# Chunked attention with a gated MLP on one core: other planned times for the w_in transfers, and a pacing limit that changes 1.5 MB later

## The chip, the cores and the metric

The kernel runs on one core of one Trainium2 chip. That core has five instruction streams that run side by side: TensorE (PE, matrix products), VectorE (DVE), ScalarE (ACT), GpSimd (POOL) and SyncE (SP, which here only issues transfers). Transfers between the chip's memory (HBM) and the on-chip buffers run on 16 DMA engines. The metric is the device time of one execution, in microseconds (us); lower is better.

## The reference

Two stages are computed, all in float32. First a chunked attention: batch 4, 8 heads, 768 positions, 64 numbers a head. Every chunk of 32 queries looks at its own 32 keys, 16 before, 8 behind, and 8 memory keys that belong to the head:

```python
scores = scale * np.matmul(q_c, k_full.transpose(0, 1, 3, 2))
scores = scores - np.max(scores, axis=-1, keepdims=True)
a = np.exp(scores)
a = a / (np.sum(a, axis=-1, keepdims=True) + 1e-09)
out[:, :, c_start:c_end] = np.matmul(a, v_full)
```

Then a gated MLP over the result x (4 x 768 x 512):

```python
h = np.maximum(x @ w_in, 0.0)                # w_in: 512 x 1024
u, v = (h[..., :d_ff // 2], h[..., d_ff // 2:])
v_n = (v - mu) / np.sqrt(var + 1e-06)        # mean and variance over v's last axis
v_s = np.einsum('ts,bsd->btd', w_spatial, v_n) + b_spatial[None, :, None]
gated = u * v_s
return (gated @ w_out).astype(np.float32)
```

The weights w_in and w_out arrive as 64-bit floats and are turned into 32-bit ones on the chip.

## The kernel before, in words

**Tiling.** The attention is cut into 24 units of 128 positions (four chunks each), all heads of a batch at once; six units make a batch. For unit i, PE forms the scores from q and a padded copy of k (`sx<-kmain,q`, L419), DVE takes the maximum and subtracts it (L476, L480), ACT takes the exponential (L485), DVE sums and inverts (L490 to L493), PE transposes the result (`pt`, L507), ACT copies it (L510), PE multiplies it by v (`sx<-vmain,pT`, L419), DVE scales (`xs`, L459), PE transposes again (`xt`, L523), and the result x is kept as a rounded high part (ACT, L528) and the rest, its low part (DVE, L532). Products of the MLP are three matmuls each, high by high, low by high and high by low (L561 to L563). Below, s2 is the score product of unit 2, mx2, p2, den2 and xs2 its steps on DVE, x2 the low part of its result, and v2 the MLP group of 12 matmuls that makes unit 2's 128 rows of v (`f<-win_h,x`); the groups that make u (`f<-x,win_h`) take three units at once.

**The weights.** w_in comes in eight pieces of 512 KB: four row blocks times two column halves (the half for v first). Each piece lands in one of four `big` buffers. Here w0 to w3 are the pieces of v's half and w4 to w7 those of u's half. A piece is converted by ACT (L864, L869), DVE (L873, L874) and POOL (L879), then split into a high part by ACT (`win_h`, L893) and a low part (`win_l`, L897) by DVE for w0 to w3 and by POOL for w4 to w7. The function `from_f64` does the conversion; it serves w_out too, whose four pieces come late in the program.

**The second half.** The normalised v and the relu of u go to HBM (`vn_far`, `u_far`) and come back for the product with w_spatial and then with w_out; both products use a scheme with seven products in place of eight (L710).

**What sets the order.** Every step is registered with the class `Plan`: its engine, an assumed duration, what it reads and writes, a rank. `Plan.order` (L76) lays all steps out in time with these assumed numbers, and the order of starts is the order of the instructions on every engine. For a transfer of mb megabytes it assumes that the one pipe for all transfers is taken for mb times drag over 0.30 us. Where PE would stand idle between 9 and 36 us of the plan, it fills the gap with matmuls on a constant (`idle<-ident`, L252), one for each 0.45 us.

**Pacing.** `held_by` (L140) says for which earlier transfer a new one waits, so that the megabytes under way stay below a limit. The same function is used for the plan and for the waits that are written into the program. Its limit is 2.0 MB until 9.0 MB have been issued, then `MIDDLE`'s 1.2 MB until 38 MB, then 1.75 MB; beyond 9.0 MB no more than eight transfers are under way either. All loads, and the stores of v and u, go through SP's one queue in program order, so a waiting transfer holds up those behind it. The third pair of q and k (for units 4 and 5) is four pieces of each.

Of the kernel before, what the change touches and what calls it, by code (L numbers as in the profile page):

```python
# [10 lines left out]
U32 = mybir.dt.uint32  # L11
# [8 lines left out]
SLOT = 40  # L20
LEFT = 16
WIN = 64
MIDDLE = (38.0, 1.2)
PIECES = 4
NEG = -1.0e30

# [1 line left out]
class Plan:  # L28
# [111 lines left out]
    def held_by(self, flight, mb, none):  # L140

        moved = sum(size for _, size in flight)
        window = self.early[1] if moved <= self.early[0] else MIDDLE[1] if moved < MIDDLE[0] else self.window
        for back, (name, size) in enumerate(reversed(flight), 1):
            mb += size
            if back == 8 and moved > self.early[0] or mb > window:
                return name
        return none
# [10 lines left out]
def tile_chunked_attention_gmlp(  # L159
# [120 lines left out]
    def transfer(e, out_, in_, mb, of=None):  # L280
        ins = e.dma_start(out=out_, in_=in_)
        made.setdefault(of, []).append(ins.ins.name)
        wait = plan.held_by(flight, mb, None)
        if wait:
            wait_for(ins, [wait], "pace")
        flight.append((ins.ins.name, mb))

    def load(dst, src_, w, rank, r=(), eng="SP", slow=1.0, us=0.45, seq=False, drag=1.0, of=None):
        e = {"SP": nc.sync, "ACT": nc.scalar, "POOL": nc.gpsimd}[eng]
        n = 4  # L290
        for s in src_.shape:
            n *= s
        mb = n / 1e6 * slow
        n = op(eng, us, lambda: transfer(e, dst() if callable(dst) else dst, src_, mb, of), r=r, w=w, rank=rank, mb=mb,
               after=line.get(eng) if seq else None, drag=drag)
        if seq:
            line[eng] = n
# [249 lines left out]
    seq = [0]  # L547
# [305 lines left out]
    def from_f64(name, src_, rank, load_rank, home, after=()):  # L853
        big = ("big", *name)
        zk = ("st", ("z", name))

        def get():
            a = alloc("big", big, [P, 2 * DH], U32).rearrange("p (c w) -> p c w", w=2)
            t_[big] = a
            return a  # L860
        load(get, src_.bitcast(U32).rearrange("p (c w) -> p c w", w=2), w=[("big", big)], r=after, rank=load_rank, seq=True)

        def scale_():
            nc.scalar.activation(alloc("st", ("z", name), [P, DH], F32), t_[big][:, :, 1].bitcast(F32), AF.Copy,  # L864
# [12 lines left out]
        def add():  # L877
# [6 lines left out]
           w=[("big", big)] if home else [zk], rank=rank)  # L884
# [17 lines left out]
    def w_in_part(c, part, rank, load_rank, sub_eng):  # L902
        cols = slice(part * DH, (part + 1) * DH)
        z, zk = from_f64(("win", c, part), w_in[c * P:(c + 1) * P, cols], rank, load_rank, False)
        split(sub_eng, DH, lambda x: (win_l if x else win_h)[:, c, cols], z, [zk], [("win", c, part)], rank)
# [31 lines left out]
    def w_out_pair(c, rank, load_rank):  # L937
        def halves(z):
            return lambda: z().rearrange("p (h n) -> p h n", h=2)

        def dst(i, x):
            third_part()
            return t_["wout"][:, i, x, c]
        (zu, ku), (zd, kd) = [from_f64(("wout", d), w_out[d * P:(d + 1) * P], 260.0, load_rank, True) for d in (c + 2, c)]
        end = [("fin", n) for n in range(count[0])]
        right_hand("wout", c, HN, halves(zu), halves(zd), [ku, *end], [kd, *end], dst, rank, "POOL", "DVE")
# [65 lines left out]
    for b in range(B + 1):  # L1012
        if b < B:
            rank = 300.0 + 10 * b
# [67 lines left out]
```

## Time and profile before

| | us |
|---|---|
| three runs | 379.18, 381.41, 376.54 |
| median | 379.18 |
| the profiled execution | 375.05 |
| its span, first to last instruction | 373.3 |
| PE busy | 355.9 (95%) |
| DVE busy | 285.0 (76%) |
| ACT busy | 187.1 (50%) |
| POOL busy | 160.5 (43%) |

The profiled execution is 4.1 us below the median of the three runs and 1.5 us below their lowest; 1.75 us of it lie outside the span. Busy times are unions over the span. The filler matmuls count as PE's busy time like any other. The granted PE clock reads full throughout. HBM moved 173 GB/s over the span.

### The profile page before, as it was taken

What the parts mean: (1) busy time and instruction counts of PE and PEld (TensorE: products, weight loads), DVE (VectorE), ACT (ScalarE), POOL (GpSimd) and SP (SyncE); (2) the same over time, 40 slices, a digit from 0 to 9 for tenths busy, and PEclk for the clock granted to TensorE, in tenths of its full rate; (3) what the DMA queues carried; (4) which work ended last, traced back from release to release, by engine and by line L of the source; (5) the groups of instructions that cost most, each with busy time, mean ns of one, the idle gap of its engine ahead of it and who ended that gap; (6) DMA issues with size and microseconds to landing.
All of it is one profiled execution on the core that took longest, in us unless ns stands there. A gap on an engine that the chain in (4) does not pass through costs nothing.

```text
span 373.3 us, 11922 instructions
## 1 busy us (share of the span) xinstructions
PE 355.9 (95%) x4988; PEld 326.7 (88%) x4988; DVE 285.0 (76%) x479; ACT 187.1 (50%) x334; POOL 160.5 (43%) x155
## 2 busy tenths in 40 slices
PE   2987989999999999999999999999999999999995
PEld 2865877998988978979889898999999999999995
DVE  3888856748758568566598589999969896898893
ACT  3768435454555454554473355346434743744371
POOL 6446642374386077520042194961256025106500
PEclk9999999999999999999999999999999999999999
DMA  8995888778787765886742648205720662230014
GB/s 230 316 260 140 232 257 210 235 217 220 228 251 214 249 212 147 274 232 194 216 163 93 246 137 311 88 2 173 246 90 3 207 217 84 84 130 2 0 54 159
DMA packets 48517, 65.52 MB, mean 176 GB/s; under 512 B 5456, under 2 KB 39888, under 8 KB 48464
## 3 DMA queue, kind: packets, MB, share of 16 engines
q1 hardware_dynamic: 47808, 64.44, 56.5%
q8 instruction: 39, 0.64, 0.8%
q10 hardware_dynamic: 656, 0.33, 0.3%
q14 instruction: 14, 0.11, 0.1%
HBM read 45.88 MB, written 18.87 MB: 173 GB/s over the span
## 4 chain that ended last, share of the span: by engine, by line
PE 83%; DVE 11%; ACT 2%; issue 2%; DMA 1%; SPq 0%; ACTq 0%; DVEq 0%
PE y L710 21%; PE f L710 15%; PE f L561 12%; PE f L562 11%; PE f L563 11%; PE sx L419 9%; PE xt L523 3%; PE pt L507 3%; DVE op L690 2%; DVE sm L673 2%; DMA k<-in_k_dram 1%; DVE st L874 1%; DVE st L873 1%; DVE wout L897 1%; DVE p L480 1%
## 5 line engine op out<-in xcount | busy, mean ns | idle before, releaser
L710 PE MATMUL y<-wsp,op 128*128 128x384 f32 x288 | 52.0, 336 | 0.9 <-ACT st L750 0.9
L764 POOL TENSOR_TENSOR ug<-st,ug 128x384 f32<-128x384 f32 x24 | 36.0, 1513 | 38.4 <-DVE st L756 34.4
L710 PEld LDWEIGHTS y<-wsp,op 128*128 128x128 f32 x288 | 49.9, 188 | 1.2 <-ACT st L750 1.2
L561 PE MATMUL f<-x,win_h 128*128 128x384 f32 x128 | 46.1, 360 | 0.0
L563 PE MATMUL f<-x,win_h 128*128 128x384 f32 x128 | 43.2, 337 | 0.0
L562 PE MATMUL f<-x,win_l 128*128 128x384 f32 x128 | 43.1, 337 | 0.0
L561 PE MATMUL f<-win_h,x 128*128 128x512 f32 x96 | 40.8, 425 | 0.0
L710 PE MATMUL f<-wsp,op 128*128 128x384 f32 x216 | 39.4, 336 | 0.0
L562 PE MATMUL f<-win_h,x 128*128 128x512 f32 x96 | 37.9, 394 | 1.0 <-DVE x L532 1.0
L563 PE MATMUL f<-win_l,x 128*128 128x512 f32 x96 | 37.7, 392 | 0.0
L710 PEld LDWEIGHTS f<-wsp,op 128*128 128x128 f32 x216 | 37.6, 188 | 0.0
L690 DVE TENSOR_TENSOR op<-sm,op 128x768 fp32r<-128x768 f32 x32 | 34.7, 1093 | 3.1 <-ACT op L687 2.6
L710 PE MATMUL y<-wout,op 128*128 128x256 f32 x288 | 35.9, 281 | 0.5 <-DVE op L690 0.5
L459 DVE TENSOR_TENSOR xs<-sx,rec 128x512 f32<-128x512 f32 x24 | 16.5, 687 | 25.1 <-PE sx L419 25.0
L710 PEld LDWEIGHTS y<-wout,op 128*128 128x128 f32 x288 | 34.7, 188 | 1.0 <-DVE op L690 0.8
L770 POOL TENSOR_TENSOR st<-st,bias 128x384 f32<-128x384 f32 x14 | 18.6, 1337 | 37.2 <-ACT st L750 28.4
L597 POOL TENSOR_TENSOR rstd<-ve,mhalf 128x1 f32<-128x1 f32 x24 | 14.7, 611 | 44.7 <-DVE ve L593 43.6
L687 ACT CAST op<-sm 128x768 fp32r<-128x768 f32 x32 | 26.2, 837 | 11.6 <-DVE sm L673 10.2
L419 PEld LDWEIGHTS sx<-kmain,q 64*32 64x32 f32 x1536 | 17.0, 107 | 14.8 <-issue 11.7
L622 ACT ACTIVATE uo<-f 128x384 f32<-128x384 f32 x32 | 15.6, 492 | 25.2 <-PE f L563 21.9
L398 POOL COPY vmain<-memv 8x1024 f32<-8x1024 f32 x22 | 23.9, 1090 | 10.0 <-PE sx L419 7.8
L419 PE MATMUL sx<-kmain,q 64*32 64x64 f32 x1536 | 20.9, 228 | 7.3 <-ACT kmain L404 7.0
(86 smaller groups left out, 770.6 us busy)
## 6 DMA issues: line engine op xcount, KB each, us to landing
vmain<-in_v_dram SPq DMA_DIRECT2D x48, 128.0 KB
vn_far<-st SPq DMA_DIRECT2D x24, 256.0 KB
u_far<-uo SPq DMA_DIRECT2D x32, 192.0 KB
vr<-vn_far SPq DMA_DIRECT2D x8, 768.0 KB
ug<-u_far SPq DMA_DIRECT2D x16, 384.0 KB
q<-in_q_dram SPq DMA_DIRECT2D x40, 128.0 KB
vmain<-in_v_dram SPq DMA_DIRECT2D x47, 96.0 KB
out_dram<-ot SPq DMA_DIRECT2D x33, 128.0 KB
```

Source lines behind the costliest of these rows:

```text
L398: ins = {"DVE": nc.vector, "POOL": nc.gpsimd}[eng].tensor_copy(to, of)
L419: ins = nc.tensor.matmul(o, w_, m, start=True, stop=True, skip_group_check=True)
L459: nc.vector.tensor_tensor(xs.rearrange("p t r d -> p r t d"), t_["sx", i][:, :, 1], rec.rearrange("p t r -> p r t").unsqueeze(3).broadcast ...
L561: nc.tensor.matmul(o, lh, rh, start=(j == 0), stop=False)
L562: nc.tensor.matmul(o, ll, rh, start=False, stop=False)
L563: nc.tensor.matmul(o, lh, rl, start=False, stop=(j == len(pairs) - 1))
L622: op("ACT", act(HT), lambda: nc.scalar.activation(alloc("uo", i, [P, HT], F32), t_["f", n], AF.Relu), r=[("f", n)], w=[("uo", i)], rank=rank)
L687: nc.scalar.copy(half(0), of())
L690: nc.vector.tensor_tensor(half(1), of(), half(0).bitcast(F32), op=ALU.subtract)
L710: nc.tensor.matmul(o, x, y, start=first and m == 1, stop=m == 3 * chunks, skip_group_check=True)
L764: nc.gpsimd.tensor_tensor(g, t_[st(x)], g, op=ALU.mult)
L770: {"DVE": nc.vector, "POOL": nc.gpsimd}[eng].tensor_tensor(a, a, bias[:, 1], op=ALU.add)
```

## The change

Two things are edited. The load of `from_f64` gets drag 0.75: the plan takes 0.524 MB x 0.75 / 0.30 = 1.31 us of the pipe for a piece of w_in or w_out, where it took 1.75. And the limit of 1.2 MB holds from 10.5 MB instead of from 9.0; between the two it is 1.75 MB. By the sizes that the plan counts, 9.05 MB have been issued when the last v of unit 3 is under way, and 10.56 MB behind the third pair of q and k and the first store of v.

```diff
-MIDDLE = (38.0, 1.2)
+MIDDLE = (10.5, 38.0, 1.2)
...
-        window = self.early[1] if moved <= self.early[0] else MIDDLE[1] if moved < MIDDLE[0] else self.window
+        window = self.early[1] if moved <= self.early[0] else MIDDLE[2] if MIDDLE[0] < moved < MIDDLE[1] else self.window
...
-        load(get, src_.bitcast(U32).rearrange("p (c w) -> p c w", w=2), w=[("big", big)], r=after, rank=load_rank, seq=True)
+        load(get, src_.bitcast(U32).rearrange("p (c w) -> p c w", w=2), w=[("big", big)], r=after, rank=load_rank, seq=True, drag=0.75)
```

No instruction of the computation is added or taken away. The order changes on every engine from the first microseconds until the last unit of attention; from the first product of the second half on, DVE's order is the same again. The first 26 transfers of SP's queue, down to the v of unit 3, stand as before; behind them the four pieces of q of the third pair now come ahead of the first store of v, which was ahead of them, and k's four pieces follow that store as they did.

On PE, at its first filler matmuls, up to the first MLP group (`idle` is the filler, `pt`, `xt` and `sx` as named above):

```order
 L419 MATMUL sx<-kmain_148,q 32x64 x32
 L507 MATMUL pt<-ident,p 128x128 x4
-L252 MATMUL idle<-ident 128x256 x13
-L507 MATMUL pt<-ident,p 128x128 x4
-L419 MATMUL sx<-vmain,pT 32x64 x32
-L252 MATMUL idle<-ident 128x256 x2
-L523 MATMUL xt<-ident,xs 128x128 x4
-L252 MATMUL idle<-ident 128x256 x3
-L419 MATMUL sx<-kmain_147,q 32x64 x32
```

In the changed program ten fillers stand at the place of the thirteen, four at the places of the two and the three, and none at the place of a single one further on: 17 in all (with three ahead of this place, the same in both) in place of 22. The first attention product now stands ahead of unit 1's transpose.

On DVE, from unit 0's x on, before (`win_l` from st_316 is w3's low part; st_442 with big_322 is w4):

```order
L532 TENSOR_TENSOR x_391<-xt_380,x_391 128x4x128
L897 TENSOR_TENSOR win_l_109<-st_316,win_h_108 128x512
L476 TENSOR_REDUCE mx_444<-sx_401 128x8
L873 TENSOR_SCALAR st_442<-st_442 128x512
L874 SCALAR_TENSOR_TENSOR st_442<-big_322,st_442 128x512
L480 TENSOR_TENSOR p_460<-sx_401,mx_444 128x2x4x64
L490 TENSOR_REDUCE den_498<-p_460 128x8
```

and in the changed program (w3 is st_313, w4 is st_431 with big_315):

```order
L532 TENSOR_TENSOR x_382<-xt_369,x_382 128x4x128
L476 TENSOR_REDUCE mx_438<-sx_397 128x8
L873 TENSOR_SCALAR st_431<-st_431 128x512
L874 SCALAR_TENSOR_TENSOR st_431<-big_315,st_431 128x512
L897 TENSOR_TENSOR win_l_109<-st_313,win_h_108 128x512
L480 TENSOR_TENSOR p_486<-sx_397,mx_438 128x2x4x64
L459 TENSOR_TENSOR xs_492<-sx_397,rec_367 128x2x4x64
L490 TENSOR_REDUCE den_503<-p_486 128x8
```

The last low part of v's half moved behind unit 2's maximum and the conversion of w4, and unit 1's xs moved ahead of unit 2's sum.

On DVE, from unit 2's xs to its x, before:

```order
L459 TENSOR_TENSOR xs_607<-sx_521,rec_501 128x2x4x64
L476 TENSOR_REDUCE mx_615<-sx_521 128x8
L601 TENSOR_SCALAR st_496<-st_496,mvar_556,rstd_604 128x512
L873 TENSOR_SCALAR st_613<-st_613 128x512
L874 SCALAR_TENSOR_TENSOR st_613<-big_449,st_613 128x512
L480 TENSOR_TENSOR p_644<-sx_521,mx_615 128x2x4x64
L532 TENSOR_TENSOR x_391<-xt_622,x_391 128x4x128
L589 BN_STATS stats_657<-st_649 128x6
```

and in the changed program:

```order
L601 TENSOR_SCALAR st_514<-st_514,mvar_556,rstd_598 128x512
L459 TENSOR_TENSOR xs_621<-sx_518,rec_506 128x2x4x64
L476 TENSOR_REDUCE mx_629<-sx_518 128x8
L873 TENSOR_SCALAR st_608<-st_608 128x512
L874 SCALAR_TENSOR_TENSOR st_608<-big_440,st_608 128x512
L480 TENSOR_TENSOR p_646<-sx_518,mx_629 128x2x4x64
L589 BN_STATS stats_651<-st_643 128x6
L591 BN_AGGR mvar_653<-stats_651 128x2
L593 TENSOR_TENSOR ve_655<-mvar_653,eps_103 128x1
L532 TENSOR_TENSOR x_382<-xt_634,x_382 128x4x128
```

The three steps of the statistics of v1 (L589 to L593) moved from behind unit 2's x to ahead of it, and the normalisation of v0 (L601) from behind unit 3's maximum to ahead of unit 2's xs.

## Rows read from the trace of the kernel before

**Rows 1.** Busy time by stretch: us, instructions; then clock, DMA share, GB/s.

```profile
core 0: us, PE busy (x) PEld busy (x) DVE busy (x) ACT busy (x) POOL busy (x), PEclk, DMA share, GB/s
8.07:24.16 16.09, 14.95 (x252) 11.82 (x247) 14.45 (x25) 11.20 (x20) 7.74 (x6) 1.00 1.04 306
24.16:41.48 17.32, 15.04 (x316) 11.37 (x311) 15.28 (x31) 11.33 (x20) 10.18 (x9) 1.00 0.70 192
...
56.00:212.00 156.00, 155.48 (x3059) 136.00 (x3058) 106.70 (x225) 79.53 (x141) 65.64 (x73) 1.00 0.71 213
212.00:228.00 16.00, 15.12 (x87) 14.75 (x86) 14.83 (x19) 8.35 (x15) 10.92 (x10) 1.00 0.57 194
```

**Rows 2.** PE's timeline, 0 to 42 us: start, us, line, [idle before <-releaser].

```profile
6.97 1.18 PE L419 MATMUL sx<-kmain,q 64*32 64x64 f32 x64 [6.97 <-ACT kmain L404]
8.07 2.93 PE L252 MATMUL idle<-ident 128*128 128x256 f32 x6
...
12.21 5.78 PE L252 MATMUL idle<-ident 128*128 128x256 f32 x26
...
21.41 0.66 PE L523 MATMUL xt<-ident,xs 128*128 128x128 f32 x4 [1.13 <-DVE xs L459]
...
24.16 0.50 PE L561 MATMUL f<-win_h,x 128*128 128x512 f32 x1
...
27.13 0.86 PE L419 MATMUL sx<-vmain,pT 64*32 64x64 f32 x64
...
37.40 0.50 PE L562 MATMUL f<-win_h,x 128*128 128x512 f32 x1 [1.01 <-DVE x L532]
...
41.48 0.34 PE L561 MATMUL f<-x,win_h 128*128 128x384 f32 x1
```

**Rows 3.** The fillers (L252) alone, in one stretch.

```profile
8.07:24.16 16.09, 11.29 (x42) 8.45 (x42) 1.00 1.04 306
```

**Rows 4.** DVE's timeline, 10 to 39 us.

```profile
10.55 0.69 DVE L490 TENSOR_REDUCE den<-p 128x8 f32<-128x512 f32 x1 [0.70 <-ACT p L485]
...
15.86 1.52 DVE L873 TENSOR_SCALAR st<-st 128x512 uint32<-128x512 uint32 x1
...
18.48 1.67 DVE L874 SCALAR_TENSOR_TENSOR st<-big,st 128x512 uint32<-128x512 uint32 x1
...
23.86 0.69 DVE L897 TENSOR_TENSOR win_l<-st,win_h 128x512 fp32r<-128x512 f32 x1 [0.32 <-ACT win_h L893]
...
27.58 0.69 DVE L490 TENSOR_REDUCE den<-p 128x8 f32<-128x512 f32 x1 [0.76 <-ACT p L485]
...
30.19 0.42 DVE L873 TENSOR_SCALAR st<-st 128x512 uint32<-128x512 uint32 x1
30.64 0.69 DVE L874 SCALAR_TENSOR_TENSOR st<-big,st 128x512 uint32<-128x512 uint32 x1
31.41 0.69 DVE L532 TENSOR_TENSOR x<-xt,x 128x512 fp32r<-128x512 f32 x1
32.80 0.69 DVE L459 TENSOR_TENSOR xs<-sx,rec 128x512 f32<-128x512 f32 x1 [0.69 <-PE sx L419]
...
36.66 0.68 DVE L532 TENSOR_TENSOR x<-xt,x 128x512 fp32r<-128x512 f32 x1
37.26 0.69 DVE L589 BATCH_NORM_STATS2 stats<-st 128x6 f32<-128x512 f32 x1
...
38.27 0.42 DVE L873 TENSOR_SCALAR st<-st 128x512 uint32<-128x512 uint32 x1
```

**Rows 5.** POOL's timeline: two of the adds of w_in.

```profile
15.38 1.72 POOL L879 TENSOR_TENSOR st<-st,big 128x512 uint32<-128x512 uint32 x1 [1.15 <-DVE st L874]
18.25 1.35 POOL L879 TENSOR_TENSOR st<-st,big 128x512 uint32<-128x512 uint32 x1 [1.15 <-DVE st L874]
```

**Rows 6.** SP's timeline around the third pair of q.

```profile
26.69 1.69 SPq L281 DMA_DIRECT2D vmain<-in_v_dram  x4
35.11 0.35 SPq L281 DMA_DIRECT2D vn_far<-st  x1
35.51 1.87 SPq L281 DMA_DIRECT2D q<-in_q_dram  x4
```

**Rows 7.** Busy time in two stretches, columns as in rows 1.

```profile
8.00:12.00 4.00, 4.00 (x83) 2.83 (x74) 2.89 (x7) 2.50 (x4) 1.83 (x2) 1.00 1.02 394
31.00:35.00 4.00, 3.04 (x67) 2.56 (x63) 3.23 (x6) 3.51 (x7) 2.61 (x3) 1.00 0.14 36
```

**Rows 8.** ACT's timeline: w4's first step; a copy of k for unit 4.

```profile
24.36 0.66 ACT L864 ACTIVATE st<-big 128x512 f32<-128x512 f32 x1
...
44.16 1.36 ACT L404 COPY kmain<-k 128x640 f32<-128x640 f32 x2
```

**Rows 9.** The chain that ended last, 212 to 228 us: start, us, what.

```profile
212.49 0.61 ACT st L585
...
223.61 1.85 DVE wout L897 x2
...
227.87 2.19 PE y L710 x11
```

## The prediction

> **What bounds the kernel now.** I read the busy times by stretch first [rows 1]. From 56 to 212 us PE is busy for 155.48 of 156.00 us, so there its amount of work sets the time, and an order that only shuffles this work can save half a microsecond at most. Between 212 and 228 us PE loses 0.88 us, and the chain that ended last runs over DVE [rows 9]: it starts at 212.49 with ACT's relu of the last v, so it moves with PE's end of the attention and keeps its length. What is left is the front, up to 41.48 us, when the groups of three units that make u begin [rows 2]. From there on PE has work in stock.
>
> In the front PE looks busy and is not: of the 14.95 us up to 24.16 us, 11.29 are fillers [rows 1, 3]. They stand where the plan saw PE waiting, so their time is waiting under another name. Who is waited for is seen in the other column: DVE is busy 14.45 of 16.09 us up to 24.16 and 15.28 of 17.32 behind it [rows 1], and PE's two marked waits end with DVE, 1.13 us on unit 0's xs and 1.01 us on the low part of unit 2's x [rows 2]. The latter is the last of the front: x2's low part ends at 36.66 + 0.68 = 37.34 us, the first matmul that needs it starts at 37.40, and 4.08 us later the group v2 is done and PE is in stock. So the question is when DVE comes to x2.
>
> From 10 us to x2, DVE is idle for 0.70 + 0.32 + 0.76 + 0.69 = 2.47 us, in four places, and it loses time to stretched instructions: an L873 took 1.52 us and an L874 took 1.67 us, against 0.42 and 0.69 for the same forms later [rows 4], so 1.10 + 0.98 = 2.08 us.
>
> **The change part by part.** *The drag of 0.75.* The plan takes 1.75 us for a piece of w_in, now 1.31. Between 8 and 12 us, when these pieces are most of what lands, the core got 394 GB/s [rows 7], at which 0.524 MB take 1.33 us; over the longer stretch to 24.16 us it was 306 GB/s [rows 1], or 1.71 us. The new number is right for the first pieces. Nothing is transferred faster by it: the first 26 transfers keep their order and their waits. What it changes is the order behind the landings, and that I cost on DVE, item by item, up to x2.
>
> - w0's conversion moves ahead of unit 0's sum, which waited 0.70 us for ACT's exponential [rows 4]. The conversion fills that hole: -0.70. If w0 lands late the hole returns; that bounds this item between -0.70 and 0.
> - w3's low part waited 0.32 us for ACT's cast [rows 4]. Unit 2's maximum and w4's conversion now stand in that hole: -0.32. The v0 group needs this low part only for its last three matmuls, so its new place costs PE nothing as long as w4 has landed.
> - Unit 1's xs moves ahead of unit 2's sum, which waited 0.76 us; an xs takes 0.69 [rows 4]: -0.69.
> - The normalisation of v0 moves ahead of unit 2's xs, which waited 0.69 us for PE [rows 4]: up to -0.69. I take -0.50, since PE's attention product of unit 2 moves too. Unit 1's x passes w5's conversion, 31.41 - 30.19 = 1.22 us [rows 4]; this is a shift between neighbours, and brings the v1 group forward without shortening DVE's list.
> - The statistics of v1 are now ahead of x2: 38.27 - 37.26 = +1.01 us [rows 4]. They did not lie before the decisive x2, and now they do; PE has nothing beside them that doesn't also wait for x2.
>
> Sum: -0.70 - 0.32 - 0.69 - 0.50 + 1.01 = **-1.20 us** at x2, and so at the end of v2. The five fillers that go are not a term of their own: their time was waiting, and the waits above are counted. The statistics of v1, once done, shorten DVE's list behind x2, but there PE is in stock.
>
> *Stretched DVE instructions.* Both stretched ones ran beside POOL's adds of w_in [rows 4, 5]: 15.86 to 17.38 us inside the add from 15.38 to 17.10, and 18.48 to 20.15 beside the one from 18.25 to 19.60. The order moves both kinds against each other, so collisions may go (-2.08) or come. I take 0, as four adds of v's half have two costly collisions in the trace and I see no reason for fewer. The Trainium skill's page "SBUF — State Buffer", section "Who interferes with whom", says that GpSimd and a VectorE instruction with both inputs in SBUF exclude each other for the whole instruction; the two rows agree, and by it each of the four adds could cost DVE up to one add, which is the third rival below.
>
> *The limit.* Between 9.05 and 10.56 MB it is 1.75 MB instead of 1.2. In the trace SP's queue stood still from 28.4 to 35.11 us, when the store of v0 went out; the loads of q behind it were issued from 35.51 [rows 6]. From 31 to 35 us the DMA share was 0.14 [rows 7]. That queue waited for the store's data, not for the limit, so the wider limit only lets q's four pieces go at once behind unit 3's v; k's follow the store, some 1.9 us earlier (the four issues of q) [rows 6]. Who uses it: ACT's copy of unit 4's k at 44.16 us, which shows no wait for it [rows 8]. PE has the v2 group and the u groups in the meantime. I cost this at 0, covered by the 4.08 us behind x2; with that cover gone it would be a gain of up to 1.9 us. w_out's drag: 0, DVE's order in the second half is unchanged.
>
> The profiled execution took 375.05 us, which becomes 373.85. That execution lies 4.13 us below the median of the runs, 379.18; against the median the forecast is 379.18 - 1.20 = **378.0 us**. Bounds for the one unknown sum: if every idle place and both collisions go and v1's statistics find cover, -2.47 - 2.08 = -4.55, 374.6 us; if no hole is filled and the statistics cost their whole time, +1.01, 380.2 us.
>
> **The rivals.** *1. The front gains more* (-2.5 to -4.5 us, about 375.7): the collisions go as well. For it: the conversions now spread more evenly among instructions that read PSUM. Against it: DVE's list up to x2 is longer by 1.01 us, and DVE already runs at 90%.
>
> *2. Nothing moves* (379.2, between -0.5 and +0.5): the change does what it says in the plan, but the reordered front is as long as before. The v1 statistics stand ahead of x2 and need the v1 group's relu, so DVE waits there and gives back what it won. The limit's half of the change does nothing in any case, since the stopped queue was waiting for data. A late w4 belongs here too: in the trace its first step ran at 24.36 us [rows 8] behind other work of ACT, so its landing is only bounded; if it isn't there by about 23 us, w3's low part and unit 2's subtraction wait behind it, one L897 or about +0.7.
>
> *3. Slower: more collisions.* The place is DVE between 11 and 22 us, where POOL adds the four pieces. Two of four cost 2.08 us, 1.04 each. If the new order lets the other two collide as well, that is +2.08 - 1.20 = +0.88, or 380.1 us. It decides as soon as more than one further add meets an L873, L874 or L897. For it: w1's and w2's conversions are now followed directly by low parts, which also read two operands on chip. Against it: the exchange brings unit 1's subtraction, which reads PSUM, behind one of them.
>
> *4. Slower: PE's clock.* With fewer fillers PE stands idle more. The first six filler records took 2.93 us, 0.49 each; the 26 later ones 5.78 us, 0.22 each [rows 2]: half the pace after a start with 6.97 us of idle time, though the granted clock of the stretch reads full [rows 7]. The wait of 1.13 us at 20.28 us did no such harm [rows 2]. Were the v0 group to run at the lower of the two levels, 1.2 in place of 2.4 GHz, its 2.97 us (24.16 to 27.13, [rows 2]) would come to twice that: +2.97 - 1.20 = +1.77, 380.95 us. The Trainium skill's page "TensorE: Matmul & The Clock Gate", section "What's actually happening", has the throttled state as the default that activity releases; by it taking fillers away is a risk, and the slow first fillers agree with it.
>
> **How the numbers follow.** Chances: forecast 0.50, rival 1 0.16, rival 2 0.18, rival 3 0.11, rival 4 0.05. The time is the forecast's, 378.0 us. The range reaches down to rival 1's bound, 374.6, and a little further, since the profiled execution shows that this program can run 4 us below its median: 374.2. Up, it takes in rivals 2 and 3, 380.2 us, and the upper half of the spread of the runs before (381.41): 381.3. By 2%, 7.6 us, which is about what a measurement of this kernel tells from no change, a gain would have to take more than half of the front's fillers and marked waits, 11.29 + 1.13 + 1.01 = 13.43 us; no case holds that. I leave 0.04 for it, and 0.03 for a loss of that size from a stall in the reordered middle that I haven't found; within 2%: 0.93.
>
> **What would show it.** Right: x2's low part on DVE ends near 36.1 us, the first u group starts near 40.3 us instead of 41.48, fillers take some 2 us less, PE is again full from 56 us to the end of the attention, and its later waits are as they were. The hole of 0.70 us ahead of unit 0's sum and that of 0.76 ahead of unit 2's are gone. Wrong: DVE idle ahead of v1's statistics (rival 2), three or four L873, L874 or L897 over 1.3 us before 24 us (rival 3), matmuls of v0 at twice their spacing of 2.97 / 12 = 0.25 us (rival 4), or a new wait of PE over 1 us behind 56 us, which none of the terms above would explain.

## The result, and the profile after

The changed kernel took 379.42 us (median of 22 runs, 375.66 to 383.34), the kernel before in the same comparison 376.57 us (22 runs, 374.79 to 381.41): a ratio of 1.0066, 95% interval 1.0043 to 1.0089. It is slower by about 2.5 us, where 1.20 us faster was forecast. The profiled execution took 377.81 us with a span of 376.0; its counterpart of before 375.05 and 373.3. Some executions of either kernel are slower than the rest as a whole (the slow state); all ratios leave them out, and of the 14 profiles below two, those with one edit alone, are of such an execution.

The busy times by stretch answer to [rows 1]. The columns are as there; two stretches around 83 us are added.

```profile
8.07:24.16 16.09, 15.26 (x247) 12.03 (x247) 15.12 (x28) 12.85 (x22) 7.51 (x6) 1.00 1.03 298
24.16:41.48 17.32, 12.91 (x303) 9.56 (x302) 15.35 (x29) 10.53 (x20) 10.58 (x10) 1.00 0.96 230
56.00:80.00 24.00, 24.00 (x582) 21.17 (x573) 18.47 (x34) 12.52 (x22) 13.61 (x13) 1.00 0.81 238
80.00:88.00 8.00, 6.26 (x26) 5.15 (x26) 3.63 (x7) 3.40 (x7) 0.92 (x2) 0.79 0.77 202
83.16:86.42 3.26, 3.26 (x11) 2.69 (x10) 1.63 (x4) 2.36 (x5) 0.00 (x0) 0.52 0.59 171
212.00:228.00 16.00, 16.00 (x90) 15.49 (x90) 14.27 (x18) 9.19 (x16) 11.40 (x10) 1.00 0.55 193
```

PE is full from 56 to 80 us, and then 8 us hold 1.74 us of idle time and a stretch in which the granted clock is 0.52, nearly all of it at the lower of the clock's two levels. PE's timeline there (start, us, line, [idle before <-releaser]):

```profile
78.52 0.80 PE L419 MATMUL sx<-kmain,q 64*32 64x64 f32 x60
...
79.18 0.82 PE L419 MATMUL sx<-vmain,pT 64*32 64x64 f32 x62
79.94 0.44 PE L561 MATMUL f<-x,win_h 128*128 128x384 f32 x1
82.11 0.33 PE L562 MATMUL f<-x,win_l 128*128 128x384 f32 x1 [1.74 <-issue]
...
84.29 0.63 PE L562 MATMUL f<-win_h,x 128*128 128x512 f32 x1
84.72 0.63 PE L563 MATMUL f<-win_l,x 128*128 128x512 f32 x1
...
86.79 0.39 PE L562 MATMUL f<-win_h,x 128*128 128x512 f32 x1
87.02 0.39 PE L563 MATMUL f<-win_l,x 128*128 128x512 f32 x1
```

The matmul at 82.11 us is the middle one of three whose operands had long been there: it waits for "issue", that is, for nothing that the profile shows. Behind it the matmuls stand 0.43 us apart (84.29, 84.72) and later 0.23 again (86.79, 87.02).

**Where the 2.7 us are.** The two profiled spans differ by 376.0 - 373.3 = 2.7 us. I gave every matmul of the program its steady spacing (0.23 us for v, 0.17 for u, 0.10 for a transpose, 0.011 for a record of an attention burst, nothing for a filler) and took what had been done by a time from that time. What is left is PE's lost time:

| up to, us | 24 | 40 | 56 | 80 | 88 | 212 | 232 |
|---|---|---|---|---|---|---|---|
| before | 19.94 | 24.43 | 27.24 | 28.07 | 28.36 | 33.61 | 34.59 |
| after | 18.09 | 24.55 | 25.79 | 26.58 | 30.21 | 36.14 | 37.19 |

The changed kernel is 1.85 us ahead at 24 us, level at 40 us, 1.49 us ahead at 80 and 1.85 us behind at 88. The loss between 80 and 88 us is 3.34 us; the wait of 1.74 and the half clock, 3.26 x (1 - 0.52) = 1.56, make 3.30 of it. Another 0.68 us goes between 88 and 212 us. And the lead of about 1.5 us at 56 us is not the forecast one, though its size is near it: the kernel before has two waits of the same kind ahead of 56 us, the changed one a single short one. These are all "issue" waits of the two timelines behind 16 us, first those of the kernel before:

```profile
31.99 0.75 PE L419 MATMUL sx<-vmain,pT 64*32 64x64 f32 x51 [0.96 <-issue]
53.42 0.32 PE L419 MATMUL sx<-vmain,pT 64*32 64x64 f32 x8 [0.90 <-issue]
136.95 0.31 PE L419 MATMUL sx<-vmain,pT 64*32 64x64 f32 x6 [0.52 <-issue]
```

and those of the changed kernel, besides the one at 82.11:

```profile
30.30 0.68 PE L419 MATMUL sx<-vmain,pT 64*32 64x64 f32 x42 [0.34 <-issue]
128.93 0.79 PE L419 MATMUL sx<-kmain,q 64*32 64x64 f32 x60 [0.48 <-issue]
140.06 0.44 PE L523 MATMUL xt<-ident,xs 128*128 128x128 f32 x2 [0.62 <-issue]
```

**What these waits are.** Count PE's instructions in the order of execution: two for each matmul record (weight load and product), one for each instruction of its sequencer. Over all 16 traces of this case 48 issue waits of 0.16 us or more stand behind 16 us, and 46 of them where this count is 192 or 193 modulo 256. (The other two, one of them the 0.48 us at 128.93 above, stay unexplained.) Such a place is called a border here, and the 256 instructions between two borders a block. The page shows who delivers at such a place, in its part on queues (packets, MB, share):

```profile
q8 instruction: 39, 0.64, 0.7%
```

39 packets of 16 KB; PE runs some 10,060 instructions, 39.3 times 256. The runs with 200 or more instructions added show 40 packets. In the packet records of the changed kernel one of them is under way from 79.45 to 80.65 us, and PE goes on at 82.11. In all 46 cases PE goes on 1.0 to 1.7 us after such a packet has landed. So PE's program comes in blocks of 256 instructions while it runs. The Trainium skill's page "Trainium Architecture — The Big Picture", section "The software stack", has instructions of 64 bytes; 256 of them are 16 KB, and the packets here have that size. An attention burst, the small matmuls of one unit's scores and another's product in one go, is 128 matmul records, 256 instructions, and PE is through it in 1.41 us. In the changed kernel unit 9's burst begins 2 places ahead of a border: the whole block is used up before the next one is there. Fetch and resumption take about 3.6 us from border to border here (1.41 + the step of 2.18 us to the next matmul). Blocks with more MLP matmuls mostly last 4 to 9 us; behind 56 us no block of this trace that lasted 4 us or more had a wait at its end. But the length of a block does not decide alone. Over all traces the packet that ended a wait started between 0.1 and 5.7 us after the last border, and many blocks of 2.5 to 3.5 us had no wait at all. No instruction within a burst was moved to do this; five fewer fillers (four instructions each), and order, moved all later bursts by some 20 places.

The front answers to [rows 2] and [rows 4]. PE, then DVE:

```profile
36.27 0.66 PE L507 MATMUL pt<-ident,p 128*128 128x128 f32 x4 [1.86 <-ACT p L485]
36.69 0.48 PE L561 MATMUL f<-win_h,x 128*128 128x512 f32 x1
37.95 0.50 PE L562 MATMUL f<-win_h,x 128*128 128x512 f32 x1 [0.79 <-DVE x L532]
...
42.92 0.45 PE L561 MATMUL f<-x,win_h 128*128 128x384 f32 x1
```

```profile
11.77 0.92 DVE L491 TENSOR_TENSOR den<-den,eps 128x8 f32<-128x8 f32 x1
...
15.66 0.92 DVE L873 TENSOR_SCALAR st<-st 128x512 uint32<-128x512 uint32 x1
...
26.01 0.69 DVE L480 TENSOR_TENSOR p<-sx,mx 128x512 f32<-128x512 f32 x1 [1.32 <-PE sx L419]
...
28.18 1.13 DVE L491 TENSOR_TENSOR den<-den,eps 128x8 f32<-128x8 f32 x1
...
35.41 0.68 DVE L589 BATCH_NORM_STATS2 stats<-st 128x6 f32<-128x512 f32 x1
36.13 0.18 DVE L591 BATCH_NORM_AGGREGATE mvar<-stats 128x2 f32<-128x6 f32 x1
36.35 0.95 DVE L593 TENSOR_TENSOR ve<-mvar,eps 128x1 f32<-128x1 f32 x1
37.22 0.68 DVE L532 TENSOR_TENSOR x<-xt,x 128x512 fp32r<-128x512 f32 x1
```

Unit 2's low part starts at 37.22 us, where before it started at 36.66 and 35.5 was forecast. A new hole of 1.32 us stands at 26 us: DVE is released by PE's attention product of 25.10 us, which itself waited 0.61 us for a load of v. And v1's statistics take 1.81 us ahead of x2. The first u group starts at 42.92 us instead of 41.48.

### The profile page after: what moved, and what is told of

It reads as the page before. It is cut to its first block, busy times and chain, and to the rows that moved or that the text cites. A ratio compares the mean times of both kernels' runs of the same rounds, so it can differ in the third digit from the quotient of the medians.

```text
span 376.0 us, 11908 instructions
## 1 busy us (share of the span) xinstructions
PE 355.7 (95%) x4978; PEld 326.7 (87%) x4978; DVE 288.5 (77%) x479; ACT 187.8 (50%) x334; POOL 160.2 (43%) x155
## 4 chain that ended last, share of the span: by engine, by line
PE 82%; DVE 8%; DMA 6%; issue 1%; ACT 1%; SPq 0%; ACTq 0%; DVEq 0%
PE y L710 21%; PE f L710 15%; PE f L561 12%; PE f L562 11%; PE f L563 11%; PE sx L419 8%; DMA q<-in_q_dram 3%; PE xt L523 3%; PE pt L507 2%; DVE op L690 2%; DMA vmain<-in_v_dram 2%; DVE sm L673 1%; DMA big<-in_moe_w_in_dram 1%; DVE wout L897 1%; DVE stats L589 1%
## 5 line engine op out<-in xcount | busy, mean ns | idle before, releaser
L561 PE MATMUL f<-win_h,x 128*128 128x512 f32 x96 | 41.2, 429 | 0.0
L562 PE MATMUL f<-win_h,x 128*128 128x512 f32 x96 | 38.3, 399 | 0.8 <-DVE x L532 0.8
```

What stands on the lines that cost most here:

```text
L561: nc.tensor.matmul(o, lh, rh, start=(j == 0), stop=False)
L562: nc.tensor.matmul(o, ll, rh, start=False, stop=False)
```

## The experiments

Theory A (A1 in the later expectations): the blocks, and what a wait for one brings on. Rival B: the changed order itself, or the lost fillers, cost the time. "Spacer matmuls" are small matmuls on a constant ahead of everything else; they change no order, only the places of all later PE instructions within the blocks. Ratios are against the kernel before on the same chip.

**Moving the kernel before by 24 instructions (before_s24).** Spacers without any other edit:

```diff
     with tc.manual_schedule(engines=set(ENGINES.values())):
+        for _ in range(6):
+            nc.tensor.matmul(idle[0:CH, 0, 0:D], ident[0:D, 0:CH], ident[0:D, 0:D], start=True, stop=True, skip_group_check=True)
         plan.emit()
```

> The kernel before with 6 such small matmuls, so every later PE instruction 24 places on. Theory A: the bursts that start at 104 and 159 us now start 2 places from a border (22 before), so both should be followed by a wait of about 1.7 us, and at least one by a stretch at half clock (1.6 us more each): 3.4 to 6.6 us, ratio 1.009 to 1.018. Theory B: no instruction of the order has moved, ratio 1.000.

382.31 us, ratio 1.0156 (1.0102 to 1.021). Two bursts now fill a block, and PE's timeline has both waits where they were expected:

```profile
107.02 0.21 PE L419 MATMUL sx<-vmain,pT 64*32 64x64 f32 x1 [2.16 <-issue]
...
166.15 0.21 PE L419 MATMUL sx<-vmain,pT 64*32 64x64 f32 x1 [1.94 <-issue]
```

The first is followed by half clock, 2.95 us of it, the second is not (same columns as the stretches above):

```profile
107.93:110.88 2.95, 2.95 (x11) 2.56 (x11) 1.58 (x4) 0.49 (x1) 0.96 (x1) 0.50 0.20 71
```

So a kernel whose order is untouched loses 1.6% by six matmuls that do nothing.

**A whole block (before_s256, then before_w256 and after_w256).** With 64 such spacers (256 instructions) all places within the blocks stay.

> The kernel before with 64 such small matmuls: 256 places, a whole block, so all borders fall where they fell. Control for the small matmuls themselves. Theory A: ratio 1.000 (0.997 to 1.003), waits of PE without a releaser where before had them (32, 53 and 137 us). If the small matmuls cost or save time by themselves (a busy PE at the start, a later first k), it shows here: up to 0.3% either way. Theory B: 1.000.

386.53 us, 1.0269 (1.0207 to 1.0331): a miss, and the spacers themselves explain it. All spacers wrote one corner of the result, so they ran one after the other, 13.75 us of them, and the first scores came at 14.86 in place of 6.97 us. It tells nothing of the blocks but that none of its waits had grown over 1.18 us. The next spacers were half-width and spread over four corners:

```diff
+        one = ident.bitcast(mybir.dt.bfloat16)
+        for j in range(128):
+            nc.tensor.matmul(idle[j % 4 * CH:j % 4 * CH + CH, 0, 0:D], one[0:D, 0:CH], one[0:D, 0:D], start=True, stop=True, skip_group_check=True)
```

> The kernel before with 256 PE instructions more at the start, a whole block: 128 one-pass matmuls of 64 columns in half-width floats on the constant, four side by side, meant to be done in under 3 us and so before the first scores at 6.97 us. Theory A: all bursts keep their places within the blocks, so the waits of PE behind instruction fetches stay at the places of the kernel before (near 32, 53 and 137 us, 0.5 to 1.2 us each) and no new one comes: ratio 1.000, within 0.003. If any added instructions did harm (a theory that only the number counts), it should cost more than the 24 instructions that gave 1.0156.

376.96 us, 1.0026 (1.0002 to 1.005), and its only issue waits stand where before has its first two:

```profile
34.11 0.74 PE L419 MATMUL sx<-vmain,pT 64*32 64x64 f32 x51 [0.17 <-issue]
55.71 0.32 PE L419 MATMUL sx<-vmain,pT 64*32 64x64 f32 x8 [0.52 <-issue]
```

256 instructions cost 0.3%, 24 cost 1.6%: the place counts, not the number. (The profiled execution is not as clean as the ratio: its block waits are shorter than before's, but PE waits 1.27 us at 28.74 and 1.48 us at 33.61 for loads of v instead.) The same on the changed kernel:

> The changed kernel with a whole block of 256 PE instructions at the start, as was done with the kernel before (1.0026). The blocks lie as in the changed kernel: A1 and A2 both want its wait back behind unit 9's burst, 1.0 to 2.2 us near 82 to 85 us, and a ratio of 1.006 to 1.011. Were the wait at 82 us an accident of the run that was profiled, it would be missing here.

379.88 us, 1.0066 (1.0021 to 1.0112), the ratio of the changed kernel itself. The wait is back at its place and longer, half clock behind it:

```profile
83.31 0.33 PE L562 MATMUL f<-x,win_l 128*128 128x384 f32 x1 [2.97 <-issue]
```

```profile
84.00:88.00 4.00, 4.00 (x15) 3.19 (x14) 1.65 (x4) 2.75 (x5) 0.00 (x0) 0.57 0.48 150
```

**Moving the changed kernel (after_s100, after_s28).** 25 spacers of the first kind:

> The changed kernel with 25 small matmuls (the shape of the score matmuls, on a constant) ahead of everything on PE, in time that PE stands idle for the first k; each is four PE instructions, so every later PE instruction stands 100 places further on. Theory A (instruction blocks): PE's program is fetched in blocks of 256 instructions; where a fused attention burst, itself 256 instructions, fills one whole block, it is through before the next block has come. In the changed kernel the burst at 78.5 us starts 2 places ahead of a block's border; with the shift the nearest burst is 12 away. So the wait of 1.74 us at 82 us and the half clock behind it go, one wait of up to 0.9 us may come elsewhere: 376 us or ratio to before 0.998 (0.994 to 1.002). Theory B (the order of work in the front costs the time, x2 behind the statistics of v1): no difference from the changed kernel, ratio 1.0066.

380.48 us, 1.0073 (1.0028 to 1.0118): a miss, and by the ratio alone it is what rival B had. The wait at 82 us was gone, but other borders now had waits: 1.86 us at 24.50, 1.03 at 103.32, 1.32 at 159.40 and 0.99 at 166.25 us (the last behind a block of more than 5 us, whose packet started 4.4 us after the border). I had asked only where whole bursts fill a block, and not how long every block lasts. For the next one I took the durations of all blocks from the trace, and seven spacers.

> The changed kernel with seven small matmuls on the constant ahead of everything (28 PE instructions), in PE's idle time at the start; the order of the rest is untouched. Theory A (PE's instructions come in blocks of 256; a block that is used up in under about 3.7 us, because it holds a whole attention burst, makes PE wait for the next one, and a long wait is followed by half clock): no burst now fills a block from its start; the short blocks are five, of about 3.45, 3.09, 2.85, 2.76 and 3.05 us, near 50, 80, 106, 135 and 161 us, so five waits of PE of at most 1.1 us at these places, none of 1.7, and the half clock behind 83 us gone: against the changed kernel as it was, -1 to -2 us, so 1.001 to 1.005 of before. Theory B (the order of the changed kernel itself, or the lost fillers, cost the 2.5 us): the wait of 1.7 us and the half clock stay near 82 us, and the ratio stays at 1.0066, within 0.003.

378.74 us, 1.0081 (1.0043 to 1.012). The part on 82 us came true (from 80 to 88 us the clock is 1.00 and PE busy 7.93 us); the time did not, and it lies where rival B had it. One wait behind 56 us was longer than thought, 1.49 us at 165.47. And this trace has half clock in the front, behind waits that have nothing to do with blocks: 0.57 from 28 to 32 us, behind 1.31 us for POOL and 0.64 for ACT, and 0.82 and 0.75 from 36 to 44, behind the wait of pt3, unit 3's transposes:

```profile
28.00:32.00 4.00, 3.68 (x127) 3.25 (x130) 3.70 (x9) 3.53 (x8) 1.82 (x2) 0.57 0.86 278
36.00:40.00 4.00, 2.11 (x15) 1.15 (x22) 3.90 (x7) 2.26 (x5) 3.63 (x4) 0.82 0.89 250
40.00:44.00 4.00, 4.00 (x77) 3.23 (x77) 2.94 (x6) 1.61 (x3) 1.69 (x4) 0.75 0.98 182
```

So A alone was too little. The mean granted clock of each execution, which the results list, says how often this happens; these are means over the runs compared: 0.997 to 0.998 for the kernel before in three comparisons (17, 29 and 26 runs), 0.993 for the changed kernel (20), 0.994 with seven spacers (7). Span times (1 - clock) is 0.6 to 1.2 us for before and 2.6 us for the changed kernel. Theory A2 adds this: uncovered waits of PE in the front, too, are followed by half clock. It can't hold for every such wait: the changed kernel's own profile has the 1.86 us at pt3 and full clock behind it:

```profile
36.00:40.00 4.00, 2.94 (x74) 2.08 (x75) 3.76 (x8) 1.32 (x3) 3.57 (x6) 1.00 0.99 230
40.00:44.00 4.00, 4.00 (x82) 3.27 (x81) 3.55 (x8) 2.82 (x5) 2.42 (x4) 1.00 0.93 186
```

**Fillers (after_f7, before_nofill_p88).** Seven fillers ahead of unit 3's transposes, at the wait of 1.86 us; the blocks behind lie as with seven spacers:

```diff
                 a = alloc("pt", i, [P, T, P], F32, psum=True)
+                if i == 3:
+                    busy(7)
                 for t in range(T):
```

> The changed kernel with seven fillers (28 PE instructions, 0.22 us each) directly ahead of unit 3's transposes (pt3), where PE stood idle for 1.4 to 1.9 us and the plan put no filler. Behind this place the bursts stand against the blocks of 256 instructions as in the run with 28 instructions at the start. Theory A1 (only the blocks cost time): no long block wait, but nothing else either: as that run, 1.005 to 1.010. Theory A2 (the blocks, and besides them PE's uncovered waits in the front, which are followed by half clock): the half clock between 36 and 44 us goes in this trace, the mean granted clock over the runs rises from 0.993 or 0.994 to above 0.996, and the ratio falls by 1 to 2 us against that run: 1.001 to 1.005. Fillers that delay pt3 themselves would cost at most 7 x 0.22 - 1.4 = 0.14 us.

378.06 us, 1.0014 (0.9978 to 1.005), mean clock 0.998, no half clock in its trace. By the plain medians, 378.06 against 376.62 us, the difference is larger, 0.4%. The block waits are much like those of the run with seven spacers (2.06 at 164.27 us, 0.44 at 107.14, and a new one of 1.16 at 31.87; there 1.49, 0.81 and 0.27). That is A2's forecast, with an error in it that speaks for A2: a filler is two records, so it takes 0.45 and not 0.22 us, and seven took 3.19 us and held pt3 up until 38.81. PE lost more time there and the ratio was still lower than with seven spacers; the two intervals overlap by 0.0007, and the two runs were on different chips.

The kernel before, with no fillers and 88 instructions of spacers in their place:

```diff
-                if spare > 0:
+                if spare > 0 and t < 10.0:
```

> The kernel before without its 22 fillers (88 PE instructions, 4 each), and with 88 PE instructions of one-pass matmuls at the start instead, so that from unit 2's first scores on every instruction stands where it stood in the blocks. The fourth rival of the prediction (and A2): waits of 1 to 6 us between 9 and 24 us are now uncovered, the clock is half for the v0 group or a stretch behind it, and the run is 1 to 3 us longer: 1.003 to 1.008, mean clock below 0.996. A1: no change, 1.000 to 1.003, as the fillers stand only where PE waits.

379.31 us, 1.0077 (1.0038 to 1.0117), mean clock 0.995. The v0 group starts at half pace, as the prediction's fourth rival had it, though the column of the granted clock reads 1.00 in this stretch:

```profile
25.37 0.63 PE L562 MATMUL f<-win_h,x 128*128 128x512 f32 x1
25.80 0.63 PE L563 MATMUL f<-win_l,x 128*128 128x512 f32 x1
26.22 0.63 PE L561 MATMUL f<-win_h,x 128*128 128x512 f32 x1
...
27.75 0.39 PE L563 MATMUL f<-win_l,x 128*128 128x512 f32 x1
27.98 0.39 PE L561 MATMUL f<-win_h,x 128*128 128x512 f32 x1
...
34.30 1.06 PE L419 MATMUL sx<-vmain,pT 64*32 64x64 f32 x51 [2.17 <-issue]
```

0.43 us apart, then 0.23. The bunched bursts also shortened a block in the front (2.97 us), so that a block wait of 2.17 us stands where the kernel before has 0.96 us, with half clock from 33.86 to 37.27 us; the run does not separate the two.

**One edit at a time (drag_only, middle_only).** The change without the limit, and without the planned times.

> The kernel before with the drag of 0.75 alone; the limit as before. 17 fillers, as in the changed kernel. Theory A: the fused burst of unit 9 starts 4 places from a border and that of unit 16 15 places ahead of one, so a wait of 1.4 to 1.7 us near 80 us, in some executions with half clock behind it: ratio 1.003 to 1.008, like the changed kernel. Theory B: as the changed kernel if the statistics of v1 stand ahead of x2 there too, else below 1.000 by up to 0.3%. Were the limit the culprit: 0.997 or less.

384.89 us, 1.0189 (1.0122 to 1.0257). The time is far above the expected one. A burst four places behind a border gives a wait where it was expected, but a longer one, and the clock behind it stays at 1.00:

```profile
87.47 0.27 PE L419 MATMUL sx<-vmain,pT 64*32 64x64 f32 x2 [2.57 <-issue]
```

There is more besides: in the profiled execution PE waits for 5.48 us at 237.59, for ACT, where the second half begins, and its clock is half from 38.88 to 45.71 and from 236.85 to 243.68 us.

> Only the limit is changed, the planned times of the weights are as before. By the argument of the prediction: same time as before (0, or up to -1.9 us), since the queue waited for the store's data. Theory A: the order moves the bursts against the blocks too; short blocks of about 3.2, 3.2, 2.5, 2.9 and 2.3 us near 50, 103, 132, 157 and 185 us, no burst that fills a block; waits of 0.5 to 1.5 us there, in sum about 2 us more than before: ratio 1.003 to 1.008. If the limit itself costs nothing in the front, unit 2's low part and the first group of u stand where they stood before, within 0.5 us.

379.84 us, 1.0089 (1.0061 to 1.0116), a little above the expected range. The waits on blocks at 110 and 196 us are 0.66 and 0.52; one at 33.85 us, not expected, is 2.90 us, with a clock of 0.57 from 32 to 40 us. Each edit alone is slower than both together. With other orders go other places in the blocks, so the effects of the edits don't add, and the limit's own worth can't be read from these runs. What happened at 237 us was not followed up.

**Putting the statistics behind x2 (after_stat1_s212 and three more).** In the plan v1's statistics also wait for unit 2's low part, and 212 instructions of half-width spacers put the borders at the best place by the trace's durations:

```diff
-        op("DVE", 1.08, stat, r=[k_], w=[("ve", i)], rank=rank, shared=True)
+        op("DVE", 1.08, stat, r=[k_, *([("x", 0, 2, "l")] if i == 1 else [])], w=[("ve", i)], rank=rank, shared=True)
```

> Two edits on the changed kernel: in the plan the statistics of v1 wait for unit 2's low part, so that DVE does that low part first (the order of PE, ACT and DVE up to there is otherwise the same), and 106 one-pass matmuls (212 PE instructions) ahead of everything put the borders of the blocks at the best place that the durations give. The prediction's term of +1.01 us for v1's statistics, if right: unit 2's low part starts near 36.0 us instead of 37.22, and PE's wait of 0.79 us for it goes; the first group of u starts near 41.9 instead of 42.92 us. Theory A: short blocks of 2.2 to 2.9, 2.8, 2.8 and 3.6 us near 57, 86, 142 and 166 us, no wait over 1.5 us behind 60 us, no half clock: 0.995 to 1.000 of before. Theory B: 1.003 or more, as the order behind 42 us is that of the changed kernel.

376.60 us, 1.0005 (0.9971 to 1.0039); run a second time 377.08 us, 0.9989 (0.9955 to 1.0023).

> The neighbour without the wide fillers, run again beside it on one chip: ratio 0.997 to 1.004 as before, with a mean clock of 0.995; A2 wants part of its runs below 0.996 in clock, with the half clock in the front.

In the first profile x2 comes 1.52 us earlier than in the changed kernel, and v2's second matmul no longer waits (it was at 37.95):

```profile
34.94 0.68 DVE L480 TENSOR_TENSOR p<-sx,mx 128x512 f32<-128x512 f32 x1
35.70 0.69 DVE L532 TENSOR_TENSOR x<-xt,x 128x512 fp32r<-128x512 f32 x1
```

```profile
37.13 0.39 PE L562 MATMUL f<-win_h,x 128*128 128x512 f32 x1
...
42.14 0.86 PE L419 MATMUL sx<-kmain,q 64*32 64x64 f32 x64 [0.87 <-ACT kmain L404]
42.92 0.45 PE L561 MATMUL f<-x,win_h 128*128 128x384 f32 x1
```

But u starts at 42.92 as before, since unit 4's scores now wait for k. This execution has no issue wait, a clock of 0.999 and took 373.11 us, 1.9 us less than the profiled one of before. The second profile of the same program took 2.54 us more at one border in the front, in a block that lasted 4.26 us (4.48 in the first, with no wait), and half clock followed:

```profile
34.49 0.64 PE L419 MATMUL sx<-vmain,pT 64*32 64x64 f32 x20 [2.54 <-issue]
```

```profile
35.97:40.50 4.53, 4.53 (x12) 3.36 (x12) 3.11 (x4) 0.44 (x1) 2.86 (x3) 0.50 0.71 218
```

Between the two lies the fetch of a block. In the first PE passes the border at 25.78 us and the packet is under way from 27.58 to 29.04; in the second PE passes it 1.70 us later, at 27.48, and the packet from 31.84 to 32.82. So of the 4.26 us by which the packet starts later, 1.70 are PE's own delay and the rest is a later start of the fetch, 4.35 against 1.80 us after the border. Mean clock over both runs of this program: 0.994. Two attempts to make its first, full-clock execution the rule:

> The run with v1's statistics behind unit 2's low part, with five fillers (20 PE instructions) ahead of pt3 and 196 in place of 212 instructions at the start, so that the blocks lie nearly as they did there (four places on). Theory A2: its runs at full clock, 371.4 us of span, become the rule, since the wait of 1.87 us ahead of pt3 is covered but for 0.8 us: mean clock above 0.997 in place of 0.995, ratio 0.993 to 0.998. Theory A1: no change against that run, 1.0005 within 0.003.

377.18 us, 0.9993 (0.9957 to 1.003): the ratio is no better than without the fillers, a miss, with a block wait of 2.84 us at 34.84 and half clock in the trace.

> The changed kernel with v1's statistics behind unit 2's low part, three wide fillers of 512 columns (some 0.44 us and 4 PE instructions each) ahead of pt3, where PE waited for 1.87 us, and 200 instructions at the start. From pt3 on the blocks lie as in the run with 212 at the start, ahead of it by 12 instructions otherwise, which leaves blocks of 4.3 us or more there. Theory A2: no wait for a block above 0.5 us, no half clock: the runs cluster at that run's full-clock spans, 371.3 to 372.2 us, and the ratio is 0.992 to 0.997, so better than both kernels. A1: as its neighbour, 1.0005 within 0.003.

381.93 us, 1.0148 (1.0111 to 1.0184): a clear miss. A wait of 3.39 us at 35.58 us, behind a block of 4.24 us, half clock from 36 to 40, and three wide fillers that took 2.74 us instead of 1.3, for the reason told above. A version that beats both kernels was not found.

**Does the order itself cost anything?** No run isolates rival B, but the traces can be set against each other. From each profiled span I take all issue waits behind 16 us and half of the time that PE worked at half clock (ahead of 360 us). For the kernel before that is 373.3 - 2.4 - 0 = 370.9 us, for the changed kernel 376.0 - 3.2 - 1.7 = 371.1. The runs before_s24, after_s100, after_s28, after_w256 and the four with the statistics behind x2 come to 370.7 to 371.5 us as well, though their spans differ by 8.5 us. By this estimate, from one trace of each, the changed order costs some 0.2 us and the rest is blocks and clock. The other six lie higher: three have edits that cost time of their own (before_s256 with 13.75 us of spacers, after_f7, before_nofill_p88), two are those with one edit alone and lose time in the second half, and before_w256 has the waits for v told above.

## Why the prediction was wrong

**The step that failed** is the one on the stretch from 56 to 212 us: "an order that only shuffles this work can save half a microsecond at most", and, from 41.48 us on, "PE has work in stock". I took PE's full row as a bound that order can't touch in either direction, but for a chance of 0.03 for a loss of 2% from a stall there "that I haven't found". Work in stock does not help an engine that has no instructions: 3.3 us were lost between 80 and 88 us with operands ready, more than the whole net loss of 2.7. The sign named for it, a new wait of PE over 1 us behind 56 us, is the 1.74 us at 82.11. The three waits of 0.5 to 0.96 us "for issue" were in the trace of before, at equal places modulo 256; the prediction does not mention them.

**The second step that failed** is the sum at x2 and its way to u: the first u group was to start near 40.3 us and started at 42.92. The next paragraph has its terms. The lead of 1.49 us at 80 us looks like the forecast 1.20 and is not: the two block waits of before in the front, 0.96 and 0.90 us, had become one of 0.34.

**The time.** 379.42 us is near the forecast 378.0 and within its range by luck: the median of three runs that it started from, 379.18, lies 2.6 us above that of the 22 runs of the comparison, 376.57.

**x2.** Forecast -1.20 us, measured +0.56 (37.22 against 36.66). *Holes:* of the four, 2.47 us, all is filled but 0.16 us and the 0.23 us that w0's conversion, moved there, waits itself; but new ones came, 1.32 us at 26.01 the largest, so idle time from 10 us on fell by 0.60 and not by 2.21. *Statistics:* they cost 1.81, not 1.01 us, because the L593 took 0.95 in place of 0.16; with them behind x2, it started 1.52 us earlier in the one profile without a long wait ahead of it, which is near this term. *Stretched instructions:* taken at 0; the long L873, L874 and L601 of before (1.10 + 0.98 + 0.54) became 0.75 and 0.96 on two L491 and 0.50 on an L873, so -0.4. Sum about -0.6 + 1.8 - 0.4 = +0.8, near the 0.56. Of the two rows that the prediction sets beside the rule on two inputs, only the L874 has two tensor inputs; the L873 has one, and it ended 0.28 us behind the add that it was said to lie inside.

**The limit,** costed at nothing, did what was said: q's four pieces went at 30.77 instead of 35.51 us and unit 4's k was copied at 40.52 instead of 44.16. In the trace that copy still waited 2.40 us for its load. Whether the limit is worth anything stays open.

**The fillers** were "not a term of their own". Their time is waiting, that held; but they seem to be worth more than it: without them all, +0.8% and half pace in v0, though a block wait and its half clock are in these 0.8%. Fewer of them also shift the program in the blocks.

**The rivals.** Rivals 1 and 2 are out by the ratio. Rival 3's collisions, stretched DVE instructions beside POOL's, number three above 0.7 us up to x2 (0.75, 0.96, 0.79) where before had two, on other instructions than it named; x2's delay is partly theirs, but no L873, L874 or L897 took over 1.3 us. Rival 4 had the mechanism, half clock behind uncovered waits, and I gave it 0.05. In the profiled execution it is not in v0 (its matmuls from 22.49 us stand 0.23 apart) but behind the block wait. The Trainium skill's page "TensorE: Matmul & The Clock Gate", section "What's actually happening", with the throttled state as the default, agrees with v0's 0.43 us between matmuls where the fillers ahead of it were gone. From span times (1 - clock), the clock is 1.4 to 2.0 us of the difference between the kernels; that is an estimate from the runs' mean clocks, those of the kernel before being from the later comparisons. In the profiled pair it is 1.7 of 2.7 us (half of the whole stretch at half clock, 83.30 to 86.71 us), and the issue waits, 3.2 us against 2.4, are 0.8, so the clock is the larger part of the net loss. The three executions of the changed kernel with a mean clock of 0.998 or more took 375.66 to 377.28 us.

**The end.** Between 212 and 228 us nothing changed: the chain again runs over DVE to the first y, at 230.40 in place of 227.87 us [rows 9].

**What stays open:** why one wait of some 2 us is followed by half clock and another (1.94 us at 166.15 with 24 instructions, 2.06 us at 164.27 with seven fillers, 2.57 us at 87.47 with the drag alone) is not; why a fetch starts 1.80 us after its border in one execution and 4.35 in another (the loads around it are not shown to be the reason: the DMA share was 1.14 from 26 to 28 us in the quick case, 0.93 and 0.92 from 28 to 32 us in the slow one); and the loss at 237 us with one edit alone.

## What to carry to other kernels

Where many tiny matmuls stand together, count PE's instructions: a border that comes to lie in front of them can make PE wait, and any edit upstream, even of a filler, moves it. Before a change of order is judged by a per cent, shift the kernel before by a few instructions and see what that alone does; here it was 1.6%. And an "issue" wait of half a microsecond that returns at a fixed count is a mechanism, not noise.

## What the runs showed of the hardware

- PE waits at places 256 instructions apart, if a block was used up too soon: 1.41 us of block gave 1.74 and 2.97 us of wait, 1.52 gave 2.16, 1.58 gave 1.94, 1.70 gave 2.57. Behind 56 us the longest wait after a block of over 4.4 us was 0.99 us (after_s100 at 166.25); in the front, where loads are dense, blocks of 4.24, 4.26 and 4.59 us gave 3.39, 2.54 and 1.86.
- A packet of 16 KB took 0.9 to 2.3 us to land, over all 16 traces; where PE waited for it, PE went on 1.0 to 1.7 us after it, and it had started 0.1 to 5.7 us after the last border.
- Of twelve block waits of 1.74 to 3.39 us nine went with 3 to 6 us of PE's work at half clock, most of it behind the wait; those of 1.94, 2.06 and 2.57 us did not.
- Half pace can stand beside a granted clock of 1.00: 0.43 us between v0's matmuls from 25.37 us on, after waits of 1.3 to 5.0 us between 17 and 24 us (before_nofill_p88).
